# A transformer block on one core: the order of every engine from tables, seven more quads on VectorE, the last tile's normalised state made turned

## The chip, the cores and the metric

The kernel runs on one core of one Trainium2 chip. A core has five engines that run their own instruction queues and wait for one another by semaphores: TensorE (PE in the profile, with its weight loads as PEld), VectorE (DVE), ScalarE (ACT), GpSimd (POOL) and SyncE (SP, which issues most DMAs). The metric is the device time of one execution in microseconds (us); lower is better.

## The reference

A block of a transformer over 2048 tokens of width 640, all in bf16:

```python
h  = x + attention(layernorm(x))          # 32 query heads of 20, one shared key and value head
h2 = h + mlp(layernorm(h))                # width 1536
# attention: q = xn @ wq ; k = xn @ wk ; v = xn @ wv
#   p = softmax(q k^T * 20**-0.5) ; o = p v ; o @ wo
# mlp: (gelu(xn @ w_gate) * (xn @ w_up)) @ w_down    (gelu in its tanh form)
```

The layer norms have no weights and an epsilon of 1e-5. There is no mask: each of 32 heads forms 2048 × 2048 scores, and every score needs one exponential.

## The kernel before

**Tiles and passes.** The 2048 tokens are 16 tiles of 128. For each tile two passes of 16 heads follow. A pass works over 16 key tiles of 128. A *unit* is one key tile against 128 queries of 4 heads that share a strip of 32 rows, that is 128 × 512 scores; four units (one for each strip) are a *quad*, so a pass has 16 quads and the kernel 512. Keys and values of all tiles are made at the start, during the first passes.

**Two ways to an exponential.** Most quads go to ScalarE: `qk_mm` (L940) makes 2 or 3 units of scores in PSUM, and one `Exp` (L1046) reads 1024 or 1536 columns and writes them to one of five buffers `pbuf`. ScalarE takes banks 0 to 2 and banks 3 to 4 in turn; such a pair is a *cycle*. `D_QUADS` names for each pass how many quads, out of the last five key tiles, go to VectorE instead. There `stream_d` makes a score product into one of two PSUM banks (5 and 7, `AUX_pool`, which the feed-forward products also use), and one VectorE instruction (L996) turns 128 × 512 scores into the bits of an approximate power of two, in int16. When a quad's four pieces stand, two shifted copies are made of it, on VectorE (L1007) or as an int32 addition on GpSimd (L1011), and all three copies, with three weights folded into copies of v (`v_w`), approximate the exponential together. So a VectorE quad costs 4 evictions and 2 shifts, and three value products on TensorE instead of one.

**Values.** The value products (L1160) of a pass gather in PSUM bank 6; the column of ones in `v_ext` yields the sums. At the end of a pass VectorE transposes the bank (L1179), takes reciprocals (L1181), and GpSimd multiplies (L1186; in the last tile VectorE does). A transposing DMA turns the heads (`onT`), then follow `wo_proj`, the second layer norm and `ffn` for this tile, spread over the passes of the next tiles. In `ffn` the gate products are copied out by VectorE (L1311), up products are evicted with a multiplication (L1319), three steps form the argument of the tanh (L1313 on GpSimd, L1322, then a whole product on VectorE or three thirds on GpSimd, L1283 and L1285), ScalarE takes the tanh (L1325), VectorE adds one (L1328), another whole or split product follows, a transposing DMA (`hhT`), and the down products. In these products (L583, `strips`) four column strips of 32 run side by side.

**The order.** Nothing of this is written as loops on the engines. `_Sched` holds a list of tasks, each with engine, dependencies, an expected length and a priority, and `schedule` plays them through in Python and so writes a fixed list for every engine. An engine carries out its list strictly in order, and `resolve` adds the semaphore waits. Strings of one digit per pass (`PATIENCE`, `MARGIN`, `URGENT`, `D_AHEAD`, `SHARE` and others) steer the choices. Value products are taken in groups: `Units.take` puts all that are ready, as far as they fit, into one row. Where TensorE would be too idle over 3.42 us, `schedule` puts in a product with zeros (`filler`, `idle`, `warm`; tile names `halves`, `zeros`).

**The last tile.** `last_tile` closes the program after the last exponential: the head outputs times wo plus x in PSUM (L1376), statistics (L1390), copies to `xh` (L1392), variance to reciprocal deviation (L1396 to L1401), the normalised tile (L1402), five transposes on TensorE (L1420) and copies (L1427); then gate and up products with the weights as the stationary side (L1445), so that h is made turned and no transpose of it is needed, Gelu on ScalarE (L1472), the product (L1477) and the down products (L1454) onto a second copy of x, and two copies out (L1488). Sums of probabilities are checked in between (L1225 to L1241); should they be out of range, a second program after a branch does everything again in a safe way, which does not happen with these inputs.

## Time and profile before

| | |
|---|---|
| three timed runs | 754.59, 761.18 and 761.88 us; median 761.18 us |
| profiled execution | 757.13 us, its span 755.8 us |
| busy time | ScalarE 724.4, TensorE 719.4, VectorE 667.9, GpSimd 271.7 us |
| mean granted TensorE clock | 0.993 of full speed |
| exponentials on ScalarE | 656 instructions, 696.6 us |
| evictions and shifts on VectorE | 532 in 350.2 us and 216 in 147.6 us |
| shifts on GpSimd | 50 in 97.3 us |

How to read it: a group's row gives line, engine and operation, what is written from what, shape and type, count, then busy time in us and the mean of one instruction in ns, then the idle time of that engine just before these instructions, and what ended it. Neighbours on one engine can overlap by some tens of ns, so that count times mean can be more than the busy time. Ends of matmuls are modelled, so that a busy TensorE is not one at its peak. A timeline row gives start and length in us, then the same names, the count of neighbours that were merged, and in brackets idle time and what ended it.

### The profile page before, as it was taken

What the parts mean: (1) busy time and instruction counts of PE and PEld (TensorE: products, weight loads), DVE (VectorE), ACT (ScalarE), POOL (GpSimd) and SP (SyncE); (2) the same over time, 40 slices, a digit from 0 to 9 for tenths busy, and PEclk for the clock granted to TensorE, in tenths of its full rate; (3) what the DMA queues carried; (4) which work ended last, traced back from release to release, by engine and by line L of the source; (5) the groups of instructions that cost most, each with busy time, mean ns of one, the idle gap of its engine ahead of it and who ended that gap; (6) DMA issues with size and microseconds to landing.
All of it is one profiled execution on the core that took longest, in us unless ns stands there. A gap on an engine that the chain in (4) does not pass through costs nothing.

```text
span 755.8 us, 24045 instructions
## 1 busy us (share of the span) xinstructions
PE 719.4 (95%) x10730; PEld 260.0 (34%) x10730; DVE 667.9 (88%) x1245; ACT 724.4 (96%) x698; POOL 271.7 (36%) x291
## 2 busy tenths in 40 slices
PE   9898999999998999999999999999999989999987
PEld 4422233333332333333333323333342323323336
DVE  8789999999998889999998899999989899888963
ACT  6999999999999999999999999999999999999982
POOL 5431315225355254324563234423232532450220
PEclk9999999999999999999999999999999999999999
DMA  7667002010113012111201102201130111010110
GB/s 181 128 218 192 10 10 45 11 30 6 31 33 45 19 23 43 27 30 10 45 3 40 33 11 46 41 20 24 23 55 20 16 20 23 19 31 19 35 33 20
DMA packets 79952, 31.53 MB, mean 42 GB/s; under 512 B 70880, under 2 KB 78560, under 8 KB 79840
## 3 DMA queue, kind: packets, MB, share of 16 engines
q1 hardware_dynamic: 78528, 29.86, 18.6%
q8 instruction: 85, 1.39, 0.7%
q10 hardware_dynamic: 1312, 0.05, 0.1%
q14 instruction: 27, 0.22, 0.1%
HBM read 10.21 MB, written 2.62 MB: 17 GB/s over the span
## 4 chain that ended last, share of the span: by engine, by line
ACT 44%; PE 41%; DVE 9%; DMA 3%; POOL 1%; issue 1%; SPq 0%; DVEq 0%
ACT pbuf L1046 42%; PE ps L583 15%; PE ps L940 14%; PE ps L1160 11%; DVE dbuf L996 3%; DVE dbuf L1007 2%; DMA onT<-oN 2%; ACT g_z L1325 1%; PE ps L1445 1%; DMA xh<-in_A_x_dram 1%; DMA xnT<-xn_tmp 1%; DVE stats L680 1%; DVE xn_tmp L703 1%; DVE stats L682 1%; POOL g_us L1285 0%
## 5 line engine op out<-in xcount | busy, mean ns | idle before, releaser
L1046 ACT ACTIVATE pbuf<-ps 128x1024 bf16<-128x1024 f32 (+1 forms) x656 | 696.6, 1218 | 9.6 <-PE ps L940 8.2
L996 DVE TENSOR_SCALAR dbuf<-ps 128x512 int16<-128x512 f32 x532 | 350.2, 680 | 40.5 <-PE ps L940 36.7
L940 PE MATMUL ps<-qT,kT 32*128 32x512 bf16 x2048 | 281.7, 387 | 16.9 <-ACT pbuf L1046 11.2
L940 PEld LDWEIGHTS ps<-qT,kT 32*128 32x128 bf16 x2048 | 73.6, 91 | 255.6 <-ACT pbuf L1046 189.7
L1007 DVE TENSOR_SCALAR dbuf<-dbuf 128x2048 int16<-128x2048 int16 x216 | 147.6, 700 | 0.8
L1160 PE MATMUL ps<-pbuf,v_ext 128*32 128x512 bf16 (+3 forms) x2052 | 144.5, 331 | 2.7 <-ACT pbuf L1046 1.7
L1160 PE MATMUL ps<-dbuf,v_w 128*32 128x512 bf16 x1596 | 139.6, 383 | 4.6 <-DVE dbuf L1007 3.3
L1011 POOL TENSOR_TENSOR dbuf<-dbuf,shifts 128x1024 int32<-128x1024 int32 x50 | 97.3, 1954 | 100.6 <-DVE dbuf L996 100.6
L1313 POOL TENSOR_TENSOR g_z<-g_gs 128x512 bf16<-128x512 bf16 x45 | 49.5, 1101 | 122.4 <-DVE g_gs L1311 122.1
L583 PE MATMUL ps<-wg_sb,xnT 128*32 128x512 bf16 x900 | 71.1, 389 | 0.5 <-DVE dbuf L996 0.2
L1160 PEld LDWEIGHTS ps<-pbuf,v_ext 128*32 128x32 bf16 x2052 | 44.9, 95 | 70.7 <-issue 49.2
L583 PE MATMUL ps<-wd_sb,hhT 128*32 128x320 bf16 x1440 | 67.6, 301 | 0.1
L583 PE MATMUL ps<-wu_sb,xnT 128*32 128x512 bf16 x900 | 66.8, 382 | 0.5 <-DVE dbuf L996 0.4
L1160 PEld LDWEIGHTS ps<-dbuf,v_w 128*32 128x32 bf16 x1596 | 39.5, 95 | 42.8 <-DVE dbuf L1007 15.7
L1285 POOL TENSOR_TENSOR g_us<-g_z,g_us 128x512 bf16<-128x512 bf16 x30 | 34.6, 1178 | 38.3 <-DVE g_z L1328 33.3
L1186 POOL TENSOR_TENSOR oN<-oT,rL 128x320 bf16<-128x320 f32 x30 | 21.8, 728 | 63.1 <-DVE rL L1181 63.0
L686 POOL CAST lnvb<-mv 128x1 bf16<-128x1 f32 x31 | 9.7, 313 | 96.0 <-DVE mv L684 95.9
L583 PEld LDWEIGHTS ps<-wd_sb,hhT 128*32 128x32 bf16 x1440 | 31.9, 96 | 25.3 <-issue 15.3
L1319 DVE SCALAR_TENSOR_TENSOR g_us<-ps,g_gs 128x512 bf16<-128x512 f32 x45 | 30.6, 679 | 6.0 <-PE ps L583 5.9
L1285 POOL TENSOR_TENSOR g_z<-g_z,g_gs 128x512 bf16<-128x512 bf16 x24 | 27.5, 1172 | 19.7 <-DVE g_z L1322 19.7
L583 PE MATMUL ps<-wo_sb,onT 128*32 128x320 bf16 x600 | 30.3, 304 | 4.5 <-DMA onT<-oN 3.8
L1311 DVE CAST g_gs<-ps 128x512 bf16<-128x512 f32 x45 | 30.5, 678 | 3.0 <-PE ps L583 2.7
(99 smaller groups left out, 407.9 us busy)
## 6 DMA issues: line engine op xcount, KB each, us to landing
out_dram<-xh SPq DMA_DIRECT2D x15, 160.0 KB, 2.1
wg_sb<-in_B_w_gate_dram SPq DMA_DIRECT2D x1, 1920.0 KB, 10.6
wu_sb<-in_B_w_up_dram SPq DMA_DIRECT2D x1, 1920.0 KB, 15.0
wd_sb<-in_B_w_down_dram SPq DMA_DIRECT2D x1, 1920.0 KB, 19.7
xh<-in_A_x_dram SPq DMA_DIRECT2D x2, 640.0 KB, 6.7
xh<-in_A_x_dram SPq DMA_DIRECT2D x3, 320.0 KB, 3.3
wq_sb<-in_A_wq_dram SPq DMA_DIRECT2D x2, 400.0 KB, 4.4
wo_sb<-in_A_wo_dram SPq DMA_DIRECT2D x1, 800.0 KB, 5.8
```

Source lines behind the costliest of these rows:

```text
L583: ins = e.matmul(out[r, :], lhs[:, r], rhs, start=start, stop=stop, tile_position=(0, 32 * b))
L940: return e.matmul(bk.rearrange("p (g n) -> p g n", g=4), kT4[r, kt * P:(kt + 1) * P], qT[r, main_q[t].index, 4 * h:4 * h + 4, :], start=Tr ...
L996: quad["bits"].append(sc.add("dve", lambda e: e.tensor_scalar(part(seg, w=slice(512 * item[0], 512 * item[0] + 512)), bk(), D_BIAS, 0.0, A ...
L1007: dep = [sc.add("dve", lambda e, j=j, s=s: e.tensor_scalar(part(s), part(seg), D_SHIFT[j], None, ALU.add), 0.602, bits + t_shift, prio=0.4 ...
L1011: dep[0].other = (lambda e, j=j, s=s: e.tensor_tensor(pairs(s), pairs(seg), shifts[:, j - 1:j].to_broadcast([P, 1024]), ALU.add), 2.03)
L1046: exps.append(sc.add("act", lambda e, w0=w0, w1=w1, to=to: e.activation(pbuf[:, to:to + w1 - w0], ps[:, w0:w1], ACT.Exp, scale=EXP_SCALE), ...
L1160: ins = e.matmul(ps[32 * b:32 * b + 32, PVB * 512 + a:PVB * 512 + a + n].rearrange("p (a n) -> p a n", n=32), x[2], span.rearrange("p (a n ...
L1186: onorm[(t, h)] = c = sc.add(by, lambda e: e.tensor_tensor(oN[:, otk.index, h * (D // 2):(h + 1) * (D // 2)].rearrange("p (g l d) -> p l g ...
L1285: return [sc.add("pool", lambda e, c=slice(512 * j, 512 * j + 512): e.tensor_tensor(out[:, k.index, c], a[:, k.index, c], b[:, k.index, c] ...
L1311: ge = sc.add("dve", lambda e, col=col, bk=bk: e.tensor_copy(g_gs[:, gsl.index, col], bk()), d_ps(512), [gm], prio=EVAC + pr, rel=[ax], na ...
L1313: sqt = sc.add("pool", lambda e, col=col: e.tensor_tensor(g_z[:, gsl.index, col], g_gs[:, gsl.index, col], g_gs[:, gsl.index, col], ALU.mult),
L1319: uts.append(sc.add("dve", lambda e, col=col, bk=bk: e.scalar_tensor_tensor(g_us[:, gsl.index, col], bk(), 0.5, g_gs[:, gsl.index, col], A ...
```

## The change

Seven quads more go to VectorE (133 to 140). The schedule that `_Sched` makes is no longer the last word: value products are first split into single pieces, then every engine's list is permuted by a table, pieces of work are moved between VectorE and GpSimd, the heads of VectorE's score products are named anew, and 54 products with zeros that the new plan contains are left out. Afterwards the list is played through once more, and the two PSUM banks of `AUX_pool` are given in the new order. The strings that steer the schedule have new values throughout.

```diff
+MOVES = {
+    "sp": (
+        "000000000100010000002000320220000121221001110101000110010110221110112012011042212220102100001000"
...
+LEFT = {
+    "off dve": (
+        "Z1VB7Z2hBbZ2tGrGZ1g6Z3u361Z11Z2R71"
+    ),
+    "off pool": (
+        "Z1DaAq9cg72821"
+    ),
+    "unused": (
...
+HEADS = (
...
+ORDER = {e: unpacked(t) for e, t in MOVES.items()}
+ORDER.update((k, places(t)) for k, t in LEFT.items())
+ORDER["heads"] = [int(c) for c in HEADS]
...
+    def split(self):
...
+            for i, x in enumerate(t.parts):
+                u = t
+                if i < len(t.parts) - 1:
+                    u = self.add("pe", None, 0.2165, [], name="pv", cfg="col")
...
+    def reorder(self, moves):
+        for t, hl in zip([t for t in self.order["pe"] if t.item is not None], moves.get("heads", [])):
+            t.item[0] = hl
+            t.groups = (hl,)
...
+        drop = [self.order["pe"][i] for i in moves.get("unused", [])]
+        assert all(t.name == "filler" for t in drop)
+        self.order["pe"] = [t for t in self.order["pe"] if t not in drop]
+        for e in self.ENGINES:
+            old = self.order[e]
+            at = moves.get(e) or range(len(old))
+            self.order[e] = [old[i] for i in at]
...
-    D_QUADS = "05554545454445445445445345453533"
+    D_QUADS = "05555455555555545555445444344434"
...
-    _DEBUG["end"] = sc.schedule()
+    sc.schedule()
+    sc.split()
+    sc.reorder(ORDER)
+    _DEBUG["end"] = sc.retime(AUX_pool)
```

In the layer norms the copy of the variance (L686) is left out, and epsilon is added to the variance itself.

The last tile takes another way. The sum x + o·wo is now formed twice, once as before and once turned, with wo as the stationary side. Since the mean over the 640 columns of that sum is linear, it is made by TensorE too: x is centred ahead of time (`centred`), and the row sums of wo (`output_means`, five reductions on VectorE) make a matrix `wo_mean` whose product with the heads is the negative mean of their part. The turned tile minus its mean goes into the gate and up products without the reciprocal deviation; this factor is spread over the rows of a tile `rows` by two small products with a diagonal, multiplied in before Gelu (`gs`) and once more, for the up side and the residual, in the last additions (`fin`, now on VectorE).

```diff
+        for c0, c1 in ((0, 3), (3, ND)):
+            hts.append(add("pe", wo_turned(c0, c1, 2, ND), 0.171 * (c1 - c0), [ha, on1], after=hts[-1:], name=f"hb{c0}_{t}"))
+            hcs.append(add("dve", lambda e, c0=c0, c1=c1: e.tensor_tensor(
+                xnT[:, c0:c1, tok], bank(c0 // 3)[:, 0:(c1 - c0) * P].rearrange("p (c n) -> p c n", n=P),
+                negm[:].unsqueeze(1).to_broadcast([P, c1 - c0, P]), ALU.add), d_ps((c1 - c0) * P),
...
-        nm = add("dve", lambda e: e.tensor_scalar(xn_tmp[:, xs.index, :], xh[:, t, :], mean(), one(lnr), ALU.subtract,
-                                                  ALU.mult), 0.45, [rc, ag] + ev, acq=[xs], rel=[ln], name=f"bnm_{t}")
-        again = add("pe", res, 0.3, ev + st, name=f"again_{t}")
...
+            gs = add("dve", lambda e, col=col, g_bk=g_bk: e.tensor_tensor(
+                g_z[:, gsl.index, col].rearrange("p (f n) -> p f n", n=P), g_bk().rearrange("p (f n) -> p f n", n=P),
+                rows[:].unsqueeze(1).to_broadcast([P, 4, P]), ALU.mult), 0.61, [gm, rwe], acq=[gsl] if i == 0 else [],
...
+            fin = add("dve", lambda e, j=j, c0=c0, c1=c1: e.scalar_tensor_tensor(
+                xh[:, t, c0:c1], acc(j), one(lnr), xh[:, t, c0:c1], ALU.mult, ALU.add), 0.41,
```

What the two programs hold, counted engine by engine up to the end of the normal path (instructions of the second, safe program left out):

| engine, operation | before | after |
|---|---|---|
| ScalarE exponentials of 1024 / 1536 columns | 452 / 204 | 447 / 198 |
| VectorE evictions of scores (L996) | 532 | 560 |
| shifts on VectorE / GpSimd | 216 / 50 | 213 / 67 |
| whole products of the feed-forward on VectorE (L1283) | 12 | 17 |
| thirds of such products on GpSimd (L1285) | 54 | 39 |
| value products with `v_w`, strips of 512 | 1596 | 1680 |
| products with zeros, strips of 512 / 256 | 188 / 0 | 136 / 40 |

In the order of the new program the tanh of tile 14 stands behind the last exponential on ScalarE; so its z product, its addition of one, its three thirds on GpSimd, the transposing DMA and its 96 down strips stand there too. On VectorE the order after the last closing transpose is: reciprocal, a check, normalised heads, z product of tile 14, a check, copy of the turned heads, an up eviction, a check, the addition of one, the two evictions of the turned tile, statistics.

More of the change, by code (lines that the diff above doesn't have):

```diff
@@ L70 @@
                  "extra", "sem", "val", "needed", "know", "pos", "lag", "cfg", "after", "opens", "rides",
-                 "groups", "late", "spare", "held", "act", "hold", "warms", "serve", "phase", "port", "issue", "other")
+                 "groups", "late", "spare", "held", "act", "hold", "warms", "serve", "phase", "port", "issue", "other", "core", "parts", "first", "last", "item", "mates", "soft")
 class _Sched:
@@ L922, in bass_sequential_preLN__grouped_kv_mqa__glu_gated_geglu__prompt_kernel @@
             also = [(n, 0) for n in range(n0, n1 + 1) if (n, 0) not in d_of]
-            assert more <= len(also)
+            if more > len(also):
+                also = sorted(also + [(n, 3) for n in range(n0, n1 + 1) if (n, 3) not in d_of and cycles[n][1]])
+            assert more <= len(also), (i, more, len(also))
             own = sorted(own + [also[(2 * i + 1) * len(also) // (2 * more)] for i in range(more)])
```

507 lines of the change are left out of this document (405 added, 102 removed).

## The prediction

> **What bounds the kernel now.** I read the busy times first, then the costliest groups, then windows of the start, of two parts of the long middle and of the tail, and the groups of the first middle window (its last row here). Columns of a window row: length, then busy time and (x instructions) of PE, PEld, DVE, ACT and POOL, granted TensorE clock, DMA share, GB/s.
>
> ```profile
> PE 719.4 (95%) x10730; PEld 260.0 (34%) x10730; DVE 667.9 (88%) x1245; ACT 724.4 (96%) x698; POOL 271.7 (36%) x291
> ACT 44%; PE 41%; DVE 9%; DMA 3%; POOL 1%; issue 1%; SPq 0%; DVEq 0%
> L1046 ACT ACTIVATE pbuf<-ps 128x1024 bf16<-128x1024 f32 (+1 forms) x656 | 696.6, 1218 | 9.6 <-PE ps L940 8.2
> L996 DVE TENSOR_SCALAR dbuf<-ps 128x512 int16<-128x512 f32 x532 | 350.2, 680 | 40.5 <-PE ps L940 36.7
> L1007 DVE TENSOR_SCALAR dbuf<-dbuf 128x2048 int16<-128x2048 int16 x216 | 147.6, 700 | 0.8
> ```
> ```profile
> 0.00:40.00 40.00, 35.64 (x521) 16.99 (x525) 30.10 (x118) 32.09 (x41) 20.45 (x66) 1.00 0.69 146
> 150.00:460.00 310.00, 301.59 (x4529) 105.02 (x4533) 284.61 (x505) 306.58 (x290) 127.59 (x113) 0.99 0.14 26
> 460.00:735.00 275.00, 261.58 (x3996) 91.01 (x3989) 242.34 (x421) 270.57 (x255) 90.64 (x84) 0.99 0.15 29
> 735.00:755.80 20.80, 16.95 (x263) 12.74 (x263) 7.67 (x22) 5.49 (x10) 0.55 (x1) 1.00 0.06 20
> ...
> L996 DVE TENSOR_SCALAR dbuf<-ps 128x512 int16<-128x512 f32 x245 | 161.4, 680 | 17.0 <-PE ps L940 15.1
> ```
>
> ScalarE's exponentials (L1046) are the longest load, and in both middle windows ScalarE is idle for only 3.4 and 4.4 us. That makes it the bound, but VectorE is close behind: 284.6 of 310 us (92%) and 242.3 of 275 us (88%). Its 25.4 us of idle time in the first window are mostly waits for score products: 17.0 us of it stands ahead of L996, 15.1 of that ended by PE L940.
>
> The 310 us window is tiles 3 to 9 (from the transpose that closes tile 2's second pass to tile 9's), the 275 us window tiles 10 to 15. I treat them apart, because the new table of quads does: summed by tile, tiles 3 to 9 go from 61 to 69 quads, tiles 10 to 15 from 48 to 47, tiles 0 to 2 stay at 24.
>
> **The change part by part.**
>
> *Seven more quads (133 to 140).* ScalarE's 656 instructions cover 2048 − 532 = 1516 units of 512 scores, so one unit costs 696.6 / 1516 = 0.46 us. Twenty-eight units leave: −12.9 us over the kernel, of which −14.7 in tiles 3 to 9 (32 units) and +1.8 in tiles 10 to 15 (4 units more).
>
> VectorE takes them. What one piece costs there when the next stands ready:
>
> ```profile
> 280.25 0.68 DVE L1311 CAST g_gs<-ps 128x512 bf16<-128x512 f32 x1
> 280.85 1.28 DVE L996 TENSOR_SCALAR dbuf<-ps 128x512 int16<-128x512 f32 x2
> 282.05 0.68 DVE L1007 TENSOR_SCALAR dbuf<-dbuf 128x2048 int16<-128x2048 int16 x1
> L1283 DVE TENSOR_TENSOR g_z<-g_z,g_gs 128x1536 bf16<-128x1536 bf16 x7 | 6.6, 946 | 0.0
> L680 DVE BATCH_NORM_STATS2 stats<-xh 128x6 f32<-128x320 bf16 x31 | 14.9, 482 | 2.7 <-DMA xh<-in_A_x_dram 2.6
> L1229 DVE TENSOR_REDUCE okay_all<-wk 128x1 f32<-128x496 bf16 x1 | 0.7, 655 | 0.0
> ```
>
> One takes 0.68 us and two take 1.28, so a piece in a full queue costs 0.60. Counting the built order between the same closing transposes, tiles 3 to 9 get 32 more evictions (244 to 276), 6 more shifts (96 to 102) and 2 more whole products (3 to 5): 38 × 0.60 + 2 × 0.87 (0.946 less the same 0.08 of overlap) = **+24.5 us** of VectorE. Tiles 10 to 15 get 6 evictions and 4 shifts fewer, 2 products more and five row sums of wo: −6.0 + 1.7 + 5 × (0.48 to 0.85) = 0 within 2. The row sum is not in this trace; its bounds are L680 (320 wide) and L1229 stretched from 496 to 640 columns; I take 0.75, nearer to the reduction. It stands in a window with 33 us of VectorE idle, so it costs nothing on the path unless that idle is used up.
>
> Now the 310 us window. The timeline marks 45 idle spells of VectorE over 0.15 us in it (first and last below) and there are as many shorter ones.
>
> ```profile
> 153.52 1.29 DVE L996 TENSOR_SCALAR dbuf<-ps 128x512 int16<-128x512 f32 x2 [0.16 <-PE ps L940]
> ...
> 457.56 0.49 DVE L807 CAST q_tok<-ps 128x320 bf16<-128x320 f32 x1 [0.37 <-PE ps L583]
> ```
>
> Ahead of each of these 90 a piece shows a tail of 0.08 us that a full queue would overlap: 7 of the 284.6 us, so the true work is about 278. After the change it is 278 + 24.5 = **302.5**, while ScalarE alone would need 310 − 14.7 = 295.3. VectorE becomes the bound of these tiles. So they cannot fall to 295; they end at 302.5 plus whatever VectorE still waits. I take 1.5 us of waiting (a full queue of evictions hides most waits for score products): 304, **−6 us**. The ends: 302.5 (−7.5), and 302.5 + 25.4 + 7 = 335 if all waits and tails stay (+25).
>
> *Tiles 10 to 15.* ScalarE: +1.8 for four units. Tile 14's tanh moves behind the last exponential: −1.4 here (row below, 1.57 with 0.20 overlapped by the next). ScalarE can also be ahead when VectorE lets go at tile 9: five exponential buffers of one cycle each, two instructions of 1.22 us (L1046's mean) per cycle, are 12 us at most; I take 5. Its 4.4 us idle I reduce by 1. Sum **−5.6**; ends −16 and 0.
>
> *Single pieces instead of groups.* Splitting the value products into one row per quad adds waits on PE, not work; 21 more groups for v_w and 7 fewer for v_ext are 14 × 0.23 = +3 us of PE by the starts of two neighbours below, spread over 700 us. Heads are exchanged so that a VectorE score product runs beside another head's; that only takes PE time out. PE has about 8 of 310 us idle by its row, though ends of matmuls are modelled, so I cost both at 0 ± 3.
>
> ```profile
> 233.59 0.40 PE L1160 MATMUL ps<-pbuf,v_ext 128*32 128x512 bf16 x4
> 233.82 0.39 PE L1160 MATMUL ps<-dbuf,v_w 128*32 128x512 bf16 x4
> ```
>
> *Zero products.* The 54 left out are taken from the new plan, not from the old program. Program against program, 47 groups of four become 34, and 10 half groups appear in the tail. What they protect:
>
> ```profile
> 241.00:244.50 3.50, 1.54 (x32) 0.54 (x22) 1.23 (x3) 1.63 (x3) 3.40 (x2) 1.00 0.46 85
> 244.50:248.00 3.50, 3.50 (x32) 0.81 (x32) 2.45 (x5) 2.73 (x3) 0.00 (x0) 0.51 0.00 0
> 613.00:616.50 3.50, 2.34 (x25) 0.61 (x24) 3.50 (x7) 3.42 (x3) 0.00 (x0) 1.00 0.24 47
> 616.50:620.00 3.50, 3.13 (x31) 0.76 (x35) 2.98 (x6) 2.60 (x4) 0.00 (x0) 0.52 0.03 7
> 664.50:668.00 3.50, 3.50 (x30) 0.49 (x22) 1.96 (x5) 2.92 (x4) 3.50 (x4) 0.53 0.02 5
> ```
>
> Three times the clock fell to half for 3.4 us. Each costs ScalarE 3.5 − 2.92 to 3.5 − 2.60, 0.6 to 0.9 us. The stretches ahead of the first two had PE busy for 1.54 and 2.34 of 3.5 us. I take 0, for VectorE's denser queue feeds PE more evenly; thirteen groups fewer at 0.9 each are the other end, +12.
>
> The Trainium skill, "TensorE: Matmul & The Clock Gate", section "What's actually happening", says that the clock halves after at least one idle window of about 3.4 us. By that rule no group removed here would matter, since no PE gap of that length stands in the middle part; this trace differs, with half speed after a stretch that was 2.34 of 3.5 us busy, and the rows decide.
>
> *The tail.*
>
> ```profile
> 725.17 1.57 ACT L1325 ACTIVATE g_z<-g_z 128x1536 bf16<-128x1536 bf16 x1
> 726.54 7.99 ACT L1046 ACTIVATE pbuf<-ps 128x1024 bf16<-128x1024 f32 x7
> 736.07 0.49 DVE L1186 TENSOR_TENSOR oN<-oT,rL 128x320 bf16<-128x320 f32 x1
> 740.05 1.27 PE L583 MATMUL ps<-wd_sb,hhT 128*32 128x320 bf16 x32
> 742.59 1.29 PE L1445 MATMUL ps<-xnT,wg_sb 128*128 128x128 bf16 x20 [0.39 <-DVE xnT L1427]
> 747.07 1.25 PE L1454 MATMUL ps<-wd_sb,hhT 128*128 128x320 bf16 x8
> 750.38 2.34 PE L1454 MATMUL ps<-wd_sb,hhT 128*128 128x320 bf16 x16
> L1285 POOL TENSOR_TENSOR g_us<-g_z,g_us 128x512 bf16<-128x512 bf16 x30 | 34.6, 1178 | 38.3 <-DVE g_z L1328 33.3
> hhT<-g_us SPq DMA_TRANSPOSE x15, 3.8
> ```
>
> The last exponential ends at 734.5; call that E. Before, the first gate product starts at E+8.1 and the last down product ends at E+18.2. In between stood statistics, the normalised tile, its transposes. The turned form needs none of these ahead of the gate: normalised heads at E+2.2 (2.0 before, a 0.17 us check moved in front). But the new order then puts tile 14's own second half here: z product 0.95 (E+3.1), tanh 1.6 (E+4.8), the +1 of 0.56 (E+5.4) and only then the two evictions that make the turned tile. First gate at about **E+6.0**, 2 us earlier. Then PE is full: six jobs of 1.12 (742.59 to 747.07 holds four) reach E+12.8; tile 14's 96 down strips, of which before had only 68 behind the transposes of the heads, and all now behind the gates, take 1.27 × 3 less overlap, about 3.3: E+16.1; the own downs 1.25 + 2.34 less overlap, 3.3: **E+19.4**, 1.2 later than before. Those strips wait for three POOL products (3 × 1.18) and a transposing DMA (3.8) behind the +1: 5.4 + 3.5 + 3.8 = E+12.7, just in time. On VectorE a reduction of 0.66 stands between the two last additions: +0.6. Tail: **+1.8**; ends −2 (the earlier gate goes through to the end) and +5.6 (the transposing DMA lands one DMA, 3.8, late).
>
> **Sum.** Profiled execution 757.13 (span 755.8 and 1.3 around it): −6 − 5.6 + 1.8 = **747.3**. The three timings shown run from 754.59 to 761.88, median 761.18; the profiled one lies inside. One per cent, 7.6 us, is about that spread and about what can be told from no change. I predict 747.
>
> **The rivals.**
>
> *A: the fine order takes more waits out.* ScalarE's lead is the full 12 us instead of 5 and the tail gains its 2 us instead of losing 1.8: 747.3 − 7 − 3.8 = 736.5. For it: every queue is arranged piece by piece. Against: VectorE's 302.5 is a floor no order lowers.
>
> *B: half of VectorE's waits stay, or PE falls to half speed behind it.* Around 613 VectorE was busy 3.50 of 3.50, PE waited for its shifts, and the clock halved. Half of 32 us in tiles 3 to 9: 302.5 + 16 = 318.5 instead of 304, so 747.3 + 14.5 = 762; with twelve half-speed windows instead, 759.
>
> *C, the slower side: VectorE's queue keeps all its waits.* Place: tiles 3 to 9, evictions in fixed order behind two score banks that the feed-forward products share. Price: 335 instead of 304, so 747.3 + 31 = 778. It decides from about 23 us of remaining waits and tails on (302.5 + 23 against 304 gives 769, 1% over the median). For it: those waits are in the trace now, and a strict order makes one late piece hold all behind it. Against: an engine with spare time must wait somewhere, so those waits do not show that it can't be filled.
>
> *D: the change doesn't do what it says*, for the zero products (13 groups net, not 54). Time unchanged: it is the forecast.
>
> **How the numbers follow.** Forecast (742 to 753) 0.50; A (733 to 742) 0.20; B (754 to 765) 0.17; C 0.13. Against the median 761.2, faster by over 1% means under 753.6: nearly all of the forecast and A, 0.69; slower means over 768.8: C, 0.13; the rest 0.18. The range leaves out C and the lowest tip of A: 734 to 764.
>
> **What would show it.** Right: ScalarE's L1046 group near 684 us, VectorE over 97% busy between the closing transposes of tiles 2 and 9, that stretch about 304 us, the first gate product 6 us and the end about 23 us behind the last exponential. Wrong: that stretch under 300 or over 312 us, more than six half-speed windows, or PE waiting for the hhT transpose in the tail for over 1 us.

## The result, and the profile after

The kernel after takes 764.6 us (median of 20 runs, 762.0 to 770.3), the kernel before 756.8 us (20 runs); the ratio is 1.0097, 95% interval 1.0075 to 1.0119. The change makes the kernel 1% slower; 747 was predicted. The profiled executions stand at 763.15 and 757.13 us, 6.0 us apart, and the account below is of these two. In all that follows a time is the median of all runs of a kernel, while its ratio leaves out four slow ones (one of e4, one of e17, two of e10).

The page of the kernel after: busy times, the chain that ended last, and three of the costliest groups (busy time, mean ns of one, idle time ahead of them).

```profile
PE 717.1 (94%) x10740; PEld 271.8 (36%) x10740; DVE 699.2 (92%) x1292; ACT 716.6 (94%) x686; POOL 282.3 (37%) x263
PE 38%; ACT 35%; DVE 20%; DMA 5%; POOL 1%; issue 1%; SPq 0%
L1321 ACT ACTIVATE pbuf<-ps 128x1024 bf16<-128x1024 f32 (+1 forms) x645 | 688.3, 1171 | 17.7 <-PE ps L1215 14.8
L1271 DVE TENSOR_SCALAR dbuf<-ps 128x512 int16<-128x512 f32 x560 | 363.7, 681 | 21.0 <-PE ps L1215 18.5
L1282 DVE TENSOR_SCALAR dbuf<-dbuf 128x2048 int16<-128x2048 int16 x213 | 149.6, 719 | 0.5
```

ScalarE did lose 8 us of work (724.4 to 716.6) and VectorE took 31 (667.9 to 699.2). VectorE's share of the chain went from 9% to 20%, ScalarE's from 44% to 35%; what ScalarE no longer works it waits: 17.7 us ahead of the exponentials in place of 9.6.

The same windows of the kernel after: tiles 3 to 9, tiles 10 to 15, the tail.

```profile
148.00:461.00 313.00, 297.53 (x4500) 109.96 (x4488) 305.09 (x535) 301.64 (x284) 134.68 (x106) 0.99 0.15 27
461.00:737.00 276.00, 261.87 (x4034) 95.30 (x4032) 246.10 (x427) 269.15 (x251) 84.48 (x74) 1.00 0.14 28
737.00:760.00 23.00, 19.20 (x333) 15.46 (x330) 14.32 (x36) 5.96 (x10) 5.46 (x5) 1.00 0.16 41
```

Between the same closing transposes the account of the 6.0 us is: up to tile 2, -2.1 (150.2 to 148.1); tiles 3 to 9, +3.1 (309.4 to 312.5); tiles 10 to 15, +0.9 (275.4 to 276.3); from the last exponential (734.53 and 736.20; the closing transposes stand 0.2 us further apart) to the end of the time, +4.35 (22.60 to 26.95). What shortened the start by 2.1 us was not tested.

The waits tell for whom TensorE's score products stand. These are waits of its weight loads, which overlap matmuls, so they are far longer than TensorE's own idle time. Before, for the two releasers of score banks (us, times, longest):

```profile
PEld ps L940 <- ACT pbuf L1046: 189.7, 498, 1.4
PEld ps L940 <- DVE dbuf L996: 12.2, 35, 0.8
```

After:

```profile
PEld ps L1215 <- ACT pbuf L1321: 112.5, 283, 0.9
PEld ps L1215 <- DVE dbuf L1271: 47.7, 133, 1.4
```

The weight loads wait 77 us less for ScalarE's banks and 36 us more for VectorE's. TensorE takes its products in order, so ScalarE's next scores can stand behind such a wait; of TensorE itself the idle time ahead of score products grew from 16.9 to 25.8 us.

### The profile page after: what moved, and what is told of

The parts are those of the page before. It is cut to its first block, busy times and chain, and to the rows that moved or that the text cites. A ratio compares the mean times of both kernels' runs of the same rounds, so it can differ in the third digit from the quotient of the medians.

```text
span 759.9 us, 24095 instructions
## 1 busy us (share of the span) xinstructions
PE 717.1 (94%) x10740; PEld 271.8 (36%) x10740; DVE 699.2 (92%) x1292; ACT 716.6 (94%) x686; POOL 282.3 (37%) x263
## 4 chain that ended last, share of the span: by engine, by line
PE 38%; ACT 35%; DVE 20%; DMA 5%; POOL 1%; issue 1%; SPq 0%
ACT pbuf L1321 34%; PE ps L858 15%; PE ps L1215 11%; PE ps L1437 10%; DVE dbuf L1271 9%; DVE dbuf L1282 4%; DMA onT<-oN 2%; DMA xnT<-xn_tmp 1%; ACT g_z L1602 1%; DVE g_gs L1588 1%; DVE g_us L1596 1%; PE ps L1779 1%; DMA qT<-q_tok 1%; DVE stats L957 1%; DVE stats L955 1%
## 5 line engine op out<-in xcount | busy, mean ns | idle before, releaser
L1321 ACT ACTIVATE pbuf<-ps 128x1024 bf16<-128x1024 f32 (+1 forms) x645 | 688.3, 1171 | 17.7 <-PE ps L1215 14.8
L1271 DVE TENSOR_SCALAR dbuf<-ps 128x512 int16<-128x512 f32 x560 | 363.7, 681 | 21.0 <-PE ps L1215 18.5
L1215 PE MATMUL ps<-qT,kT 32*128 32x512 bf16 x2048 | 284.4, 385 | 25.8 <-ACT pbuf L1321 13.1
L1286 POOL TENSOR_TENSOR dbuf<-dbuf,shifts 128x1024 int32<-128x1024 int32 x67 | 129.6, 1947 | 109.7 <-DVE dbuf L1271 70.6
L1437 PE MATMUL ps<-dbuf,v_w 128*32 128x512 bf16 x1680 | 152.7, 386 | 2.9 <-DVE dbuf L1282 2.7
L1437 PE MATMUL ps<-pbuf,v_ext 128*32 128x512 bf16 (+3 forms) x1960 | 136.5, 332 | 0.3
L858 PE MATMUL ps<-wg_sb,xnT 128*32 128x512 bf16 x900 | 64.2, 382 | 1.7 <-DMA xnT<-xn_tmp 1.3
L1562 POOL TENSOR_TENSOR g_us<-g_z,g_us 128x512 bf16<-128x512 bf16 x24 | 28.4, 1203 | 40.7 <-DVE g_z L1605 31.9
L961 POOL TENSOR_SCALAR lnve<-mv 128x1 bf16<-128x1 f32 x31 | 9.9, 322 | 64.2 <-DVE mv L959 62.9
L858 PE MATMUL ps<-wq_sb,xnT 128*32 128x320 bf16 (+1 forms) x660 | 31.7, 298 | 0.7 <-DMA wq_sb<-in_A_wq_dram 0.5
```

The source lines that it names most:

```text
L858: ins = e.matmul(out[r, :], lhs[:, r], rhs, start=start, stop=stop, tile_position=(0, 32 * b))
L1215: return e.matmul(bk.rearrange("p (g n) -> p g n", g=4), kT4[r, kt * P:(kt + 1) * P], qT[r, main_q[t].index, 4 * h:4 * h + 4, :], start=Tr ...
L1271: quad["bits"].append(sc.add("dve", lambda e: e.tensor_scalar(part(seg, w=slice(512 * item[0], 512 * item[0] + 512)), bk(), D_BIAS, 0.0, A ...
L1286: dep[0].other = (lambda e, j=j, s=s: e.tensor_tensor(pairs(s), pairs(seg), shifts[:, j - 1:j].to_broadcast([P, 1024]), ALU.add), 2.03)
L1321: exps.append(sc.add("act", lambda e, w0=w0, w1=w1, to=to: e.activation(pbuf[:, to:to + w1 - w0], ps[:, w0:w1], ACT.Exp, scale=EXP_SCALE), ...
L1437: ins = e.matmul(ps[32 * b:32 * b + 32, PVB * 512 + a:PVB * 512 + a + n].rearrange("p (a n) -> p a n", n=32), x[2], span.rearrange("p (a n ...
```

## The experiments

Two theories at the start. **V**: 140 quads are too much for VectorE, and its late banks starve ScalarE. **O**: the table's order itself costs. Beside them **T**: the new last tile costs some 4 us. After e4 to e7 a further reading was needed, **F**: ScalarE and TensorE are both full in the kernel before, and the change makes VectorE the third. Against it stands **L**: the round trip between the engines in a fixed order sets the time, not the work of any.

All ratios are to the kernel before, timed on the same chip beside the kernel; the times come from several chips, so that kernels are compared by their ratios. Window columns: length of the stretches of tiles 3 to 9 and 10 to 15 in the profiled execution, between marks rounded to the us (a length can be off by up to 1).

| kernel | time, us | ratio, 95% interval | 3-9 | 10-15 |
|---|---|---|---|---|
| before | 756.8 | 1 | 310 | 275 |
| after | 764.6 | 1.0097 (1.0075-1.0119) | 313 | 276 |
| e1 after, planner's order | 796.0 | 1.0509 (1.0484-1.0534) | 335 | 277 |
| e2 before, 140 quads | 815.8 | 1.0763 (1.0740-1.0785) | 331 | 275 |
| e3 after, 133 quads, planner's order | 776.2 | 1.0231 (1.0199-1.0263) | 328 | 271 |
| e4 after, short shifts | 761.1 | 1.0050 (1.0025-1.0076) | 310 | 275 |
| e5 after, short exponentials | 763.6 | 1.0075 (1.0046-1.0104) | 314 | 276 |
| e6 after, short value products | 763.5 | 1.0076 (1.0046-1.0107) | 313 | 274 |
| e7 before, short exponentials | 754.5 | 0.9959 (0.9930-0.9988) | 308 | 275 |
| e8 after, flag ahead of the last addition | 766.4 | 1.0102 (1.0068-1.0136) | 312 | 278 |
| e9 before, exponentials and values | 744.4 | 0.9783 (0.9735-0.9831) | 306 | 269 |
| e10 after, exponentials and values | 761.5 | 1.0000 (0.9964-1.0036) | 314 | 271 |
| e11 after, all three cuts | 749.3 | 0.9873 (0.9801-0.9946) | 306 | 267 |
| e12 after, last tile mended | 763.7 | 1.0079 (1.0046-1.0112) | 313 | 277 |
| e13 the same, flag early | 769.5 | 1.0163 (1.0099-1.0227) | 312 | 276 |
| e14 before, short value products | 756.6 | 0.9988 (0.9964-1.0012) | 310 | 275 |
| e15 after, short GpSimd shifts | 760.7 | 1.0044 (1.0009-1.0078) | 308 | 278 |
| e16 after, exponentials and shifts | 758.7 | 1.0028 (0.9997-1.0059) | 308 | 273 |
| e17 after, zero products back | 770.3 | 1.0136 (1.0079-1.0193) | 317 | 275 |
| e18 after, heads not exchanged | 781.6 | 1.0291 (1.0246-1.0336) | 320 | 284 |

### The table and the quads apart: e1, e2, e3

```diff
 e1, on the kernel after
-    sc.reorder(ORDER)
+    sc.reorder({})
 e2, on the kernel before: twelve strings (D_QUADS, PATIENCE, FILL, LAG, URGENT, SHARE, H_POOL, Z_POOL ...) as in the kernel after
-    D_QUADS = "05554545454445445445445345453533"
+    D_QUADS = "05555455555555545555445444344434"
 e3, on the kernel after: no table, and those strings as in the kernel before
```

> The kernel after without its table of orders: every engine works in the order that the planner gives for the same pieces (140 quads, single value products, the new last tile). Theory O (the table's order is what costs: TensorE's strict queue holds ScalarE's scores behind VectorE's banks): 750 to 757 us, faster than the kernel after (about 764), with the stretch from tile 2's to tile 9's closing transpose under 309 us. Theory V (VectorE has too much work with 140 quads, whatever the order): 764 to 775 us, that stretch at 313 us or more. Theory T (the new end costs 4 us): no difference between the two orders at the end.

> The kernel before, its groups, its planner's order and its old last tile unchanged, with the new strings alone: 140 quads in place of 133, 28 units of 512 scores less on ScalarE. Theory V: no gain or a loss, 757 to 770 us, VectorE over 96% busy in tiles 3 to 9. If the quads are good and the table or the new end spoil them: 744 to 752 us. My prediction's own sum for tiles 3 to 15 was -11.6 us, so 745.

> The kernel after with the old strings (133 quads) and the planner's order: single value products, the turned h of the last tile and tile 14's second half behind the last exponential stay. Theory T (the new end costs about 4 us): 759 to 763 us, last exponential where it was before (about 734.5) and 25 to 27 us from it to the end of the time. If the new end is harmless: 757 us or less, 22 to 23 us from the last exponential to the end.

All three times lie above every range that was named for them. O falls at once: without its table the kernel after takes 796.0 us, so the table is worth 31 us. The table holds more than the order: e1 also lacks the exchange of heads, which alone is worth some 16 us (e18), keeps the 54 zero products, and moves no work between VectorE and GpSimd. The quads without the table are a loss of 7.6% (e2); part of that is an end left open by strings that do not fit (the last output is issued 50 us behind the last exponential, 19 in the kernel before). e3 could not isolate T as I meant it to: its end, in the planner's order, is 12 us longer than before (34.85 us from the last exponential), and its tiles 3 to 9 take 328 us. I take it that plan, strings and order are fitted to one another, and that a part taken alone shows mostly the misfit.

### One engine's work cut at a time: e4, e5, e6, e7, e14

```diff
 e4  VectorE's shift: columns part(s, w=cut(s)), 1408 of 2048 except at a buffer's first use
 e5, e7 (the same on before)
-                pbuf[:, to:to + w1 - w0], ps[:, w0:w1], ACT.Exp, scale=EXP_SCALE)
+                pbuf[:, to:to + w1 - w0 - cut], ps[:, w0:w1 - cut], ACT.Exp, scale=EXP_SCALE)
 e6, e14 (the same on before): value products of 512 columns, but the first of a pass, on 384
+                cut = lambda n: n if n < 512 or first else 384
```

> The kernel after, with VectorE's shifts by whole digits done on 1408 of 2048 columns (but for the first use of each buffer, which keeps the whole width); a part of the shifted scores is left out. Each shift loses 640 of 2048 columns, about 0.17 of 0.62 us, 35 us of VectorE in all and 17 in tiles 3 to 9; every wait, order and all of ScalarE's and TensorE's work stay. Theory V: 746 to 755 us, the stretch of tiles 3 to 9 at 300 to 306 us. Theory O (order, not VectorE's work): within 3 us of the kernel after.

> The kernel after, with every exponential from the 41st cycle on 64 columns shorter (those columns are left out); order, waits and the other engines' work unchanged. Each loses about 0.053 us, about 30 us of ScalarE in all. Theory S (ScalarE's work still sets the time of the kernel after): 736 to 745 us. Theory P (TensorE's fixed order and its own work set it, ScalarE waits): 757 to 763 us, ScalarE's idle grows by what is taken from it. Theory M (all three engines are near full and hand the time to one another): 748 to 757 us.

> The kernel after, with each value product of 512 columns but the first of its row cut to 384 columns (the rest of the keys is left out); order and waits unchanged. A piece of four goes from about 0.23 to 0.18 us; some 650 pieces, so about 30 us of TensorE. Theory P (TensorE's work sets the time): 735 to 748 us. Theory S: within 3 us of the kernel after (764). Theory M: 750 to 760 us.

> The kernel before with the same shorter exponentials, about 30 us of ScalarE less. My prediction's reading (ScalarE bounds the kernel before; VectorE, its true work 278 of the 310 us window, comes next): 727 to 740 us. If TensorE's order or work is the bound already: 750 to 757 us.

> The kernel before with the shorter value products alone. Exponentials alone gave 0.996 of the kernel before, both cuts 0.978. Theory F (ScalarE and TensorE both full in the kernel before): 0.990 to 1.000, so 750 to 759 us, since ScalarE holds the time. If TensorE alone was the bound: 0.978 to 0.985, as with both cuts.

None returns more than a quarter of what it takes away. By the pages' busy times e4 took 27 us from VectorE and won 3.5 us, e6 17 us from TensorE and won 1, e5 20 us from ScalarE and won 1. V as I had stated it missed its 746 to 755 with e4, and e5 reached none of its three ranges. e6 stayed within 3 us of the kernel after, as a bound by ScalarE alone would have it, but e5 rules that bound out. The misses that matter most are on the kernel before: 16 us less ScalarE there is worth 0.4% (e7; 727 to 740 had been expected), 13 us less TensorE nothing that can be told (e14). ScalarE alone is not the bound that I had called it.

### Two and three engines cut: e9, e10, e11, e16

> The kernel before with both cuts, the shorter exponentials (about 30 us of ScalarE) and the shorter value products (17 to 30 us of TensorE); the columns cut off are left out. The exponentials alone gave -4 us. Theory F (in the kernel before ScalarE and TensorE are both full, each hides the other's relief; VectorE has room, as my prediction had it): 733 to 742 us. Theory L (what sets the time is the round trip between the engines in a fixed order, not the work of any): 750 us or more.

> The kernel after with both cuts. Theory F, with VectorE as the third full engine in tiles 3 to 9 (98% busy there): tiles 3 to 9 stay at 306 us or more, only tiles 10 to 15 gain: 745 to 757 us. If VectorE does not bind in tiles 3 to 9: 735 to 745 us. Theory L: 758 us or more.

> The kernel after with the cuts of all three engines: exponentials, value products, and VectorE's shifts on 1408 of 2048 columns. Theory F: well below each cut alone, 732 to 744 us, tiles 3 to 9 under 300 us. Theory L: 755 us or more.

> The kernel after with the shorter exponentials and the shorter VectorE shifts, TensorE's work whole. Together with TensorE's cut it was 0.987 of the kernel before, exponentials and value products alone 1.000, shifts alone 1.005. Theory F (three full engines): TensorE holds the time, 0.995 to 1.005, 755 to 763 us. If TensorE has room: 0.985 to 0.993.

These are combinations of the same edits. In the kernel before, 0.4% and 0.1% apart become 2.2% together, 16 us: ScalarE and TensorE each hide the other's relief, and VectorE, untouched, does not. At 744.4 us e9 lies between the ranges of F and L; a gain of two cuts that is far above the sum of their single gains is what F says. e9's windows:

```profile
149.00:455.00 306.00, 295.04 (x4529) 106.24 (x4533) 283.45 (x505) 296.66 (x289) 127.47 (x113) 0.99 0.15 27
455.00:724.00 269.00, 254.46 (x3999) 91.51 (x3992) 241.98 (x422) 260.15 (x255) 90.65 (x84) 0.99 0.16 30
```

In the kernel after the same pair leaves tiles 3 to 9 at 314 us (e10), where VectorE is 302 us busy, and wins 5 us in tiles 10 to 15, where it has room. With VectorE's cut added tiles 3 to 9 fall, by 8 us (e11); that cut alone takes 3 us from them (e4). First e10, then e11:

```profile
150.00:464.00 314.00, 294.60 (x4476) 111.15 (x4472) 301.70 (x533) 289.76 (x282) 134.25 (x105) 0.97 0.15 27
464.00:735.00 271.00, 253.89 (x4041) 96.05 (x4038) 245.13 (x428) 259.47 (x252) 84.83 (x74) 1.00 0.15 29
```
```profile
149.00:455.00 306.00, 287.63 (x4497) 110.34 (x4485) 289.46 (x534) 287.82 (x283) 131.86 (x106) 0.98 0.16 28
455.00:722.00 267.00, 253.04 (x4042) 96.19 (x4043) 234.88 (x428) 258.25 (x252) 83.59 (x74) 1.00 0.15 29
```

e10 is the weakest of these: at 761.5 us it lies above F's range (745 to 757) and in L's (758 or more). Part of its 314 us is the granted clock, 0.97 over the stretch: between 280 and 290.5 and between 423.5 and 437.5 us it was 0.67 and 0.63, and 6.4 of VectorE's 12.3 us of idle time fall into these two spells. So e10 does not show that the pair wins nothing there; at a like clock it wins (last section).

I read the whole as F: VectorE binds tiles 3 to 9 of the kernel after, for its own 305 us there leave 8 of 313, with the other two right behind it. The pair without TensorE (e16) stands between, where F had put it. The times F had named were too low for e9 and e11 too (733 to 742 and 732 to 744), because I had put each cut at about 30 us: by the pages' busy times they are 22 on ScalarE and 17 on TensorE in e9, and 16 us came out; 26, 21 and 31 (VectorE) in e11, and 17 came out.

### TensorE's parts of the change undone: e17, e18

```diff
 e17: each of the 54 dropped zero products is inserted again behind the product that it followed in the plan
 e18
-    sc.reorder(ORDER)
+    sc.reorder({k: v for k, v in ORDER.items() if k != "heads"})
```

> The kernel after with the 54 left-out zero products put back, each behind the product that it followed in the plan (or at the next place where its bank is open): 54 groups of about 0.22 us, 12 us of TensorE. Theory F (TensorE is one of three full engines): +2 to +8 us on the kernel after, 766 to 772, with a granted clock of 0.998 or more. If they fall into TensorE's waits: within 2 us of the kernel after. My prediction cost leaving them out at 0, with +12 as the other end; if leaving them out was harmful, this kernel is faster than the kernel after, 755 to 762 us.

> The kernel after without the exchange of heads: VectorE's score products keep the heads that the plan gave them, order and all else unchanged. Two neighbours on one head run one behind the other (0.22 us more) in place of side by side. My prediction counted the exchange as TensorE time only, 0 plus or minus 3. Theory F: slower by 2 to 10 us, 766 to 775. If TensorE has room: within 2 us of the kernel after (764).

Groups of TensorE by form: score products and zero products of the kernel after, then of e18 and e17.

```profile
L1215 PE MATMUL ps<-qT,kT 32*128 32x512 bf16 x2048 | 284.4, 385 | 25.8 <-ACT pbuf L1321 13.1 <-DVE dbuf L1271 4.6 <-DVE g_us L1596 2.5
L858 PE MATMUL ps<-halves,zeros 128*32 128x512 bf16 x136 | 13.1, 474 | 1.1 <-DVE halves L940 1.1
```
```profile
L1215 PE MATMUL ps<-qT,kT 32*128 32x512 bf16 x2048 | 311.4, 383 | 21.2 <-ACT pbuf L1321 10.9 <-DVE dbuf L1271 3.5 <-DVE g_us L1596 1.7
```
```profile
L858 PE MATMUL ps<-halves,zeros 128*32 128x512 bf16 x348 | 30.6, 412 | 1.1 <-DVE halves L940 1.1
```

Without the exchange of heads the same 2048 products take 27 us more and the kernel 17 us more (15 by the ratios). The kernel before spends 281.7 us on them with heads of its planner's own choice, so I read the exchange as buying back what the new neighbours would have cost. F had named 766 to 775 us; 781.6 is beyond it. The zero products put 17.5 us of work back by their own group (11 by TensorE's busy time on the page, 728.3 in place of 717.1, for neighbours overlap) and cost 3 to 7 us: 0.4% of the ratio, with intervals that overlap, and 766.2 us of span at full granted clock against 758.5 to 760.6 for the kernel after. Adding work to TensorE cost a part of it that shows, 15 to 17 of 27 us in e18; taking work off it alone returned little. That is how an engine looks that is full together with others.

### GpSimd: e15

```diff
-                        pairs(s), pairs(seg), shifts[:, j - 1:j].to_broadcast([P, 1024]), ALU.add), 2.03)
+                        pairs(s)[:, 0:cut(s)], pairs(seg)[:, 0:cut(s)], shifts[:, j - 1:j].to_broadcast([P, cut(s)]), ALU.add), 2.03)
```

> The kernel after, with GpSimd's shifts on 128 of 1024 pairs of columns (but for the first use of a buffer); a part of the shifted scores is left out. Theory G (GpSimd's longer passes hold up VectorE's shifts, which is where VectorE's 305 us in tiles 3 to 9 come from in place of my 302.5): VectorE busy 1.5 to 4 us less in tiles 3 to 9, its shifts' mean 0.70 us or less in place of 0.719, the time 0 to 4 us shorter. If there is no hold-up: VectorE's busy time within 1 us, the time within 2 us of the kernel after (764).

VectorE's shifts in tiles 3 to 9 of the kernel after, then of e15, in which only GpSimd's shifts are shorter:

```profile
L1282 DVE TENSOR_SCALAR dbuf<-dbuf 128x2048 int16<-128x2048 int16 x102 | 72.5, 728 | 0.0
```
```profile
L1284 DVE TENSOR_SCALAR dbuf<-dbuf 128x2048 int16<-128x2048 int16 x102 | 69.8, 702 | 0.0
147.00:455.00 308.00, 296.25 (x4498) 110.39 (x4490) 301.71 (x534) 301.15 (x283) 80.58 (x105) 1.00 0.15 28
```

The same 102 shifts take 26 ns less each, VectorE's busy time falls from 305.1 to 301.7 us and the stretch from 313 to 308. G holds, and where VectorE binds 3.4 us of its time come with 4 to 5 of the stretch, a part of which can be the granted clock (1.00 here, 0.99 in the kernel after).

### The last tile: e8, e12, e13

```diff
 e8: okay sums, flag product and flag moved ahead of the last additions
 e12: the same, and the last tile's h in a place of its own
+    hhL = dbuf[:, 0:1, 0:NF * P].rearrange("p o (f n) -> p o f n", n=P)
+    ahead(d, [f"hh{last}_{f}" for f in (0, 4, 8, 10)] + ["ok2_0", "okb"], f"fin0_{other}")
+    ahead(pe, [f"dn{j}_{last}_{i}_0" for i in (0, 1) for j in (1, 0)], f"dn320_{other}_0")
 e13: the same, sums ahead of the reciprocal deviation, flag product in another bank, flag ahead of the first product of h
+    ahead(d, ["ok1_0", "ok2_1", "ok2_0", "okb"], f"brc_{last}")
+    ahead(d, ["flag"], f"hh{last}_0")
```

> The kernel after, with the last check sums on VectorE ahead of the last tile's products of h, TensorE's flag product ahead of its own down products and the flag ahead of the last two additions; nothing is left out. Theory T, with the flag read by the engines behind the last output as its second part: the reduction of 0.66 us no longer stands between the last two additions (-0.7 to -1.3 us), and the time outside the span falls from 3.4 to 1.3 us (-2): 761 to 762 us. If the time outside the span has another cause: 763 to 764 us.

> The kernel after with the end reordered, nothing left out: the last tile's turned h gets a place of its own (in a buffer of quads that is free by then), so VectorE's four products of it and two thirds of TensorE's own down products come ahead of the second half of tile 14's strips; the flag's sums and product come ahead of the last down products and the flag ahead of the last addition. Theory T: the end is 1.5 to 2 us earlier in the span and the time outside the span falls from 3.4 to about 2: 760 to 762 us, 3 us under the kernel after, still over the kernel before. If the strips, not the order, set the end: 763 us or more.

> The kernel of the mended last tile, with the flag's sums in VectorE's idle 2 us behind the statistics of the last tile, its product ahead of the last gate products and the flag ahead of the products of h: about 11 us behind the last exponential and 9 us ahead of the last output. From the issue of the last output to the end of the time it was 4.9 us in the kernel after, 5.0 with the mended last tile, 3.9 in the kernel before. If the late flag (read and branched on by every engine at the very end) makes this difference: 3.9 us here, so 762 to 763 us. If not: 4.9 us, 763 to 764 us.

The tail of the kernel after, E = 736.20 (start, us, engine, line, operation, count, idle time ahead and its releaser):

```profile
742.03 1.29 PE L1789 MATMUL ps<-xnT,wg_sb 128*128 128x128 bf16 x20
747.80 1.28 PE L1779 MATMUL ps<-xnT,wu_sb 128*128 128x128 bf16 x20
749.12 1.81 PE L858 MATMUL ps<-wd_sb,hhT 128*32 128x320 bf16 x48
751.53 1.81 PE L858 MATMUL ps<-wd_sb,hhT 128*32 128x320 bf16 x48 [0.60 <-DVE xh L1621]
753.39 1.95 DVE L1833 TENSOR_TENSOR hhT<-ps,g_gs 128x512 bf16<-128x512 f32 x4 [1.92 <-PE ps L858]
754.14 3.49 PE L1798 MATMUL ps<-wd_sb,hhT 128*128 128x320 bf16 x24 [0.80 <-DVE hhT L1833]
756.51 0.66 DVE L1506 TENSOR_REDUCE okay_all<-wk 128x1 f32<-128x496 bf16 x1
757.67 0.55 DVE L1847 SCALAR_TENSOR_TENSOR xh<-ps,lnr,xh 128x320 bf16<-128x320 f32 x1 [0.31 <-PE ps L1516]
758.14 0.15 DVE L1518 TENSOR_SCALAR flag<-ps 128x1 int32<-128x1 f32 x1
758.25 0.33 SPq L1850 DMA_DIRECT2D out_dram<-xh  x1
```

VectorE's four products of h waited 1.92 us for tile 14's strips, because both tiles share the one `hhT` buffer. e12 takes that wait out; its end:

```profile
750.97 1.48 DVE L1834 TENSOR_TENSOR dbuf<-ps,g_gs 128x512 bf16<-128x512 f32 x2
752.26 2.35 PE L1799 MATMUL ps<-wd_sb,dbuf 128*128 128x320 bf16 x16
756.32 1.25 PE L1799 MATMUL ps<-wd_sb,dbuf 128*128 128x320 bf16 x8
758.50 0.43 SPq L1851 DMA_DIRECT2D out_dram<-xh  x1
```

Its last exponential ends at 737.59: the last output is issued at E+20.9 in place of E+22.05. The reduction was no part of it: in e8 it is out of the way, and the last output still goes at E+22.1, since TensorE's last down products end at E+21.5.

The other part lies behind the last output. From its issue to the end of the time it is 4.9 us in the kernel after, 5.0 in e12, 4.5 in e8, 3.9 in the kernel before and 3.5 in e13, whose flag stands 8 us ahead of the last output (767.59 to 771.13). So a flag that comes last costs about 1 us there, by one profiled execution of each. Where exactly this time goes was not settled: the time outside the span is 3.25 to 3.64 us in each of the 20 runs of the kernel after and 1.33 in the profiled run before; in e8 and e12 it shrank (to 2.1 and 1.4), but the span behind the last exponential grew by 0.8 us. As whole kernels e8 and e12 are within the interval of the kernel after: neither won the 2 to 4 us that T had named. e13, for which 762 to 763 us had been named, took 769.5, and that time cannot be read for its edit: in the profiled run its start ran 10 us late at half clock (last section). Its tail, from the last exponential to the end, is 25.3 us against 26.95.

No kernel that computes everything was faster than the kernel before.

## Why the prediction was wrong, by its steps

**What bounds the kernel** is the step that failed first. I read 306.6 of 310 us on ScalarE, called it the bound and put VectorE next, and passed over the 301.6 us of TensorE in the same row because matmul ends are modelled. Taking 16 us off ScalarE gave 0.4%, taking work off both gave 2.2% (e7, e14, e9). A quad moves exponentials off ScalarE but leaves TensorE its score products and gives it three value products for one, so ScalarE's 12.9 us were never the path by themselves.

**Seven more quads.** The count of units over the kernel was right; taking 32 of them, 14.7 us, off ScalarE between these two marks was not. I counted by the tile that a quad belongs to, but the stretches are cut by time. Exponentials executed between the same transposes of tiles 2 and 9, first before, then after:

```profile
L1046 ACT ACTIVATE pbuf<-ps 128x1024 bf16<-128x1024 f32 x196 | 196.8, 1096 | 2.5 <-PE ps L940 2.3
L1046 ACT ACTIVATE pbuf<-ps 128x1536 bf16<-128x1536 f32 x86 | 131.0, 1523 | 0.9 <-PE ps L940 0.8
```
```profile
L1321 ACT ACTIVATE pbuf<-ps 128x1024 bf16<-128x1024 f32 x196 | 192.4, 1039 | 7.7 <-PE ps L1215 6.8
L1321 ACT ACTIVATE pbuf<-ps 128x1536 bf16<-128x1536 f32 x81 | 118.5, 1463 | 3.5 <-PE ps L1215 3.1
```

Five of 1536 columns fewer are 15 units, 6.9 us at my 0.46. ScalarE's own need there was by this sum 303 us, not 295.3 (its busy time is 301.6): as much as VectorE's. Of the 17 units between the two counts some 6 were left over from the start, where 6 fewer were executed, and some 10, near 5 us, were done ahead for later tiles: the lead that I had put at 5 us under tiles 10 to 15 did come, and was paid for here.

**VectorE becomes the bound of tiles 3 to 9**: right in kind (e10 against e11; 97.5% busy, over 97% was forecast), too small in size. 302.5 us of work became 305.1, and e15 gives 301.7 when GpSimd's shifts are short: the missing term is the hold-up of VectorE's shifts by GpSimd. The larger miss is the waiting, taken as 1.5 us: it was 7.9 (313 less 305.1). Three groups of VectorE there, scores, gate copies and the addition behind wo:

```profile
L1271 DVE TENSOR_SCALAR dbuf<-ps 128x512 int16<-128x512 f32 x277 | 178.4, 681 | 1.9 <-PE ps L1215 0.9
L1588 DVE CAST g_gs<-ps 128x512 bf16<-128x512 f32 x18 | 12.2, 679 | 1.1 <-PE ps L858 1.1
L1548 DVE TENSOR_TENSOR xh<-xh,ps 128x320 bf16<-128x320 bf16 x14 | 6.8, 485 | 2.3 <-PE ps L858 2.0
```

The full queue did hide the waits for scores, 17.0 us before and 1.9 now. The waits for TensorE's other products stayed: over the five groups that read them 6.4 us before and 5.5 now, where my sum had 1.5 for all waits together. Forecast 304, measured 312.5, just beyond the bound that I had named as wrong.

**Tiles 10 to 15**: -5.6 forecast, +0.9 measured. The lead came, and ScalarE executed 6 units fewer there; tile 14's tanh left the stretch, but one of an earlier tile came in, so seven stand there in either kernel. ScalarE's idle time grew from 4.5 to 7.0 us instead, mostly in waits for TensorE's scores. TensorE's busy time stayed at 262 us. I conclude that ScalarE's lead needs TensorE to run ahead as well; with both relieved this stretch does fall, by 6 us, in either kernel (e9, e10).

**Single pieces and heads** at 0 plus or minus 3: the exchange alone is worth 27 us of TensorE and some 16 us of time (e18). The sum near 0 came out by luck: TensorE's busy time hardly changed (719.4 to 717.1), but as the difference of two large terms that I had not seen.

**Zero products** at 0, with +12 if missed: they were not missed. The granted clock was 0.998 with them left out (0.993 before), and putting them back costs 3 to 7 us (e17). The reason given, that VectorE's denser queue feeds TensorE more evenly, was not tested.

**The tail**: first gate product at E+5.8 (E+6.0 forecast), last of the gate and up products done at E+12.9 (12.8). Then the strips were done at E+17.1 in place of 16.1, 0.60 of it a wait for a bank, and the own downs at E+21.4 in place of 19.4: 1 us from the strips and 0.80 of waiting for the shared `hhT` that I had not looked at. The 0.6 us for the reduction was not on the path (e8). Within the span the tail grew by 2.4 us (21.3 to 23.7), near the forecast. The other 1.9 stand outside the span, which the sum took as unchanged: about 1 goes with the flag behind the last output, and the rest stays open. Together +4.35 in place of +1.8.

**The rivals.** B's 762 lies nearest, but not by its mechanism: of 25 us of VectorE's waits 7.9 stayed, a third and not half, and the granted clock rose. C's 31 us of remaining waits did not come; D, which left the sum as it was, decided nothing. What happened, three engines full at once, was among none of them, so that B's number is luck.

## What to carry to other kernels

Two engines over 97% busy in one window, as here, can be one bound: before moving work between a third and one of them, cut each alone and then both, and read what comes back. Compare runs at a like granted clock, for a cut can change it. Count work by what is executed between two marks, not by the table that assigns it to tiles. When a fuller queue is to hide an engine's waits, ask for each group of waits whether it does. In an order as fixed as this one, work added to a full engine cost time at once while work taken from one engine returned little; whether an order made anew would return more was not tried.

## What the runs showed of the hardware

**Half clock under full load.** In e13 TensorE stood idle for 1.35 us at the start, waiting for a transposing DMA, and soon after ran at half clock for some 30 us (to 62), the first 19 of them busy without a gap (timeline row, then windows):

```profile
31.52 0.45 PE L1037 MATMUL ps<-xnT,wk 128*128 128x128 bf16 x5 [1.35 <-DMA xnT<-xn_tmp]
30.00:34.00 4.00, 2.65 (x26) 0.90 (x23) 1.44 (x8) 2.61 (x3) 0.71 (x2) 0.75 0.44 84
34.00:40.00 6.00, 6.00 (x64) 3.08 (x61) 1.16 (x4) 4.83 (x5) 0.00 (x0) 0.50 0.28 54
40.00:50.00 10.00, 10.00 (x82) 2.15 (x78) 4.92 (x10) 6.67 (x6) 4.55 (x5) 0.50 0.01 2
```

So e13 closes tile 2 10.7 us later than the kernel after, though its edit begins only in the last tile. The Trainium skill, "TensorE: Matmul & The Clock Gate", section "What's actually happening", gives full rate after at least one busy window of about 3.4 us; this trace does not fit one such window, with 16 us of full busy time at 0.50. Ends of matmuls are modelled, so that short gaps in the busy time can't be excluded.

**Cuts can lower the clock.** The eight runs of e10 behind its ratio were granted 0.980 to 0.995 and took spans of 760.9 to 753.4 us, nearly in that order; the kernel after had 0.987 to 1.000. The median over the runs behind the ratio is 0.998 for the kernel after, 0.995 with short exponentials (e5), 0.991 with short value products (e6), 0.988 with both (e10), and 1.000 with only the shifts of VectorE or GpSimd short (e4, e15). Each of e10's two spells in tiles 3 to 9 follows 3.5 us in which TensorE was 2.55 and 1.72 us busy. So part of what a cut wins goes to the clock; why some cuts lower it and others do not was not settled.

Among runs granted 0.993 the spans are 754.9 to 757.1 us for the kernel before, 753.8 with short exponentials (e7), 751.7 with short value products (e14), 741.1 and 742.8 with both (e9). For the kernel after they are 762.6 to 764.9, with short exponentials 760.5 to 762.4 (e5), with short value products 758.9 and 760.8 (e6), with both 755.0 (e10). At 0.989 the kernel after took 766.9 and e11, with all three cuts, 744.6. So at a like clock the change costs about 8 us, one cut wins 2 to 4, two 9 to 14 and three some 22 (one run of each kernel): F's pattern, and e10 is no exception to it.

**GpSimd holds VectorE up** by 26 ns in a shift of 702, averaged over 102 shifts, 37 of GpSimd's own beside them (e15). The Trainium skill, "GPSIMD Engine Reference", section "Key points", says that the two share their SBUF interfaces; the trace agrees, by 2.7 us in tiles 3 to 9. Which interface it is no run here shows.
